# LN1 with the fourth tile's sums on DVE and the first table pieces on ACT's queue; the fourth turn beside the last n1 inverse

## Chip, cores, metric

The kernel runs on one core of a Trainium2 chip. The metric is the device time of one execution in microseconds (us). Engines are named as in the profile: PE is the matrix engine (TensorE), DVE the vector engine, ACT the scalar engine, POOL is GpSimd, SP issues most DMAs.

## The reference, cut to what matters

```python
def _A_ref(x, w_r, w_i):                       # 2048 x 576, bf16
    X = jnp.fft.rfft2(x.astype(jnp.float32)) * (w_r + 1j * w_i)
    return jnp.fft.irfft2(X, s=(S, D)).astype(jnp.bfloat16)
def _B_ref(x, w_gate, w_up, w_down):
    return (gelu(x @ w_gate) * (x @ w_up)) @ w_down
h  = x + _A_ref(layernorm(x), w_r, w_i)
h2 = h + _B_ref(layernorm(h), w_gate, w_up, w_down)
```

The Fourier transforms are matrix products with tables. The scale of the first layer norm (LN1), one number per row, is multiplied into the table of the first transform instead of into x.

## The kernel before

x lies in 16 tiles of 128 rows. LN1 works in five groups of tiles (0-1, 2-3, 4-7, 8-11, 12-15). A tile's statistics come either from DVE (two `bn_stats` of 288 columns and one `bn_aggr`) or, for the tiles in `ACT_TILES`, from two passes of ACT (sum, sum of squares) and two small DVE ops on 128x1 that make a variance of them:

```python
ACT_TILES = (1, 3, 7, 11, 13)
def ln1_var(i):
    for c in range(c0, c1):
        if c in ACT_TILES:   # L446
            P.op(DVE, lambda v: v.scalar_tensor_tensor(TM[:,0,c:c+1], SA[:,0,c:c+1], 1.0/(D*D), SA[:,0,c:c+1], mult, mult) ...)
        else:                # L449
            P.op(DVE, lambda v: v.bn_aggr(MV1[:,c,:], ST1[:,c,:,:]) ...)
    for c in range(c0, c1):
        if c in ACT_TILES:   # L452
            P.op(DVE, lambda v: v.scalar_tensor_tensor(MV1[:,c,1:2], SA[:,1,c:c+1], 1.0/D, TM[:,0,c:c+1], mult, subtract) ...)
```

Then, for each group: root on ACT (`ln1_sqrt`), reciprocal on DVE (`ln1_rs`), the table tile times the scale into `ATS` (`ln1_scale`; groups 2 and 3 in one POOL op, the others on DVE), 10 or 20 matmuls into PSUM (`a_mms`), and five evictions into `U` (`a_evs`, on ACT or DVE). The next transform ("the first transform over U", line L600) needs all of them: its first three matmuls read eviction numbers 0, 1 and 2 of every group, its second half (matmuls 4 to 6) numbers 3 and 4. `idle_mm(n, i)` puts n matmuls without use ahead of group i. After the start comes the middle of the LN1 order:

```python
    # ... groups 0 and 1 cut
    ln1_var(2); ln1_sqrt(2); a_evs(1, ACT, (2, 3, 4)); ln1_tile(8)
    ln1_rs(2);  ln1_scale(2, POOL); idle_mm(7, 2); a_mms(2)
    act_sum(11); act_sq(11); ln1_tile(9); ln1_tile(10); act_sum(13)
    ln1_var(3); ln1_sqrt(3); act_sq(13); ln1_tile(12)
    ln1_rs(3);  ln1_scale(3, POOL); ln1_tile(14)
    a_evs(2, ACT, (0, 1, 2)); ln1_tile(15)
    ln1_var(4); a_evs(2, DVE, (4,)); ln1_sqrt(4); ln1_rs(4); ln1_scale(4, DVE)
    a_evs(2, ACT, (3,)); idle_mm(4, 3); a_mms(3)
    # ... evictions of group 3, a_mms(4), evictions of group 4
```

The other place is the seam between the inverse stage and the FFN. Per tile c, `st_I(c)` (six matmuls, evicted by ACT into `GS`) and `st_N(c-1)` (four matmuls, "n1 inverse") alternate; `turn_pe` transposes one of the first four normalised tiles after tiles 8, 10, 12 and 14; and the last `st_N(15)` comes after the first six FFN matmuls (line L872), which are of another shape (64 instead of 128 rows).

Of the kernel before, what the change touches and what calls it, by code (L numbers as in the profile page):

```python
# [6 lines left out]
ACTF = mybir.ActivationFunctionType  # L7
# [7 lines left out]
NT = 16  # L15
# [280 lines left out]
def _build(nc, A_x, A_w_r, A_w_i, B_w_gate, B_w_up, B_w_down, out):  # L296
    P = Prog(nc)
    T = build_tables()
    dram = {n: nc.inline_tensor(_np_bf16(T[n]), name="c_" + n.lower()) for n in T}
    PE, DVE, ACT, SP, POOL = "pe", "dve", "act", "sp", "pool"  # L300
# [41 lines left out]
    HT0 = sb.alloc("HT0", [128, 5, 512], BF16)  # L342
# [3 lines left out]
    ATB = sb.alloc("ATB", [128, NT, 128], BF16)  # L346
# [21 lines left out]
    PS = nc.alloc_psum_tensor("PS", [128, 4096], F32)  # L368
# [13 lines left out]
    tabs = dram["ATAB"].rearrange("p (c k) -> p c k", c=NT)  # L382
# [1 line left out]
    def x_load(i, c0, c1):  # L384
        P.dma(SP, XO[:, c0:c1, 0:D], xv[:, c0:c1, :], f"x{i}", w=[("X", c) for c in range(c0, c1)])

    def atb_load(i, c0, c1):
        P.dma(SP, ATB[:, c0:c1, :], tabs[:, c0:c1, :], f"atb{i}", w=[("ATB", c) for c in range(c0, c1)])

    x_load(0, 0, 2)  # L390
    x_load(1, 2, 4)
    atb_load(0, 0, 4)
    x_load(2, 4, 8)
    atb_load(1, 4, 8)
    x_load(3, 8, 12)
    x_load(4, 12, 16)
    atb_load(2, 8, 16)
# [27 lines left out]


    GROUPS = ((0, 2), (2, 4), (4, 8), (8, 12), (12, 16))
    ACT_TILES = (1, 3, 7, 11, 13)

    def act_sum(c):  # L430
        P.op(ACT, lambda a, c=c: a.activation(JNK[:, 0, :], XO[:, c, 0:D], ACTF.Identity, accum_out=SA[:, 0, c:c + 1]),
             r=[("X", c)], w=[("SA0", c), "J0"])

    def act_sq(c):
        P.op(ACT, lambda a, c=c: a.activation(JNK[:, 1, :], XO[:, c, 0:D], ACTF.Square, accum_out=SA[:, 1, c:c + 1]),
             r=[("X", c)], w=[("SA1", c), "J1"])

    def ln1_tile(c):
        for h in range(2):
            P.op(DVE, lambda v, c=c, h=h: v.bn_stats(ST1[:, c, h, :], XO[:, c, 288 * h:288 * h + 288]), r=[("X", c)], w=[("ST1", c, h)])  # L440

    def ln1_var(i):
        c0, c1 = GROUPS[i]
        for c in range(c0, c1):
            if c in ACT_TILES:
                P.op(DVE, lambda v, c=c: v.scalar_tensor_tensor(TM[:, 0, c:c + 1], SA[:, 0, c:c + 1], 1.0 / (D * D), SA[:, 0, c:c + 1],  # L446
                                                                op0=ALU.mult, op1=ALU.mult), r=[("SA0", c)], w=[("TM", c)])
            else:
                P.op(DVE, lambda v, c=c: v.bn_aggr(MV1[:, c, :], ST1[:, c, :, :]), r=[("ST1", c, 0), ("ST1", c, 1)], w=[("MV1", c)])  # L449
        for c in range(c0, c1):  # L450
            if c in ACT_TILES:
                P.op(DVE, lambda v, c=c: v.scalar_tensor_tensor(MV1[:, c, 1:2], SA[:, 1, c:c + 1], 1.0 / D, TM[:, 0, c:c + 1],  # L452
                                                                op0=ALU.mult, op1=ALU.subtract), r=[("SA1", c), ("TM", c)], w=[("MV1", c)])

    def ln1_sqrt(i):
        c0, c1 = GROUPS[i]
        P.op(ACT, lambda a, c0=c0, c1=c1: a.activation(RS1[:, c0:c1], MV1[:, c0:c1, 1], ACTF.Sqrt, bias=EPT[:, 0:1]),
             r=[("MV1", c) for c in range(c0, c1)] + ["EPT"], w=[("SD1", i)])

    def ln1_rs(i):  # L460
        c0, c1 = GROUPS[i]
        P.op(DVE, lambda v, c0=c0, c1=c1: v.reciprocal(RS1[:, c0:c1], RS1[:, c0:c1]), r=[("SD1", i)], w=[("RS1", i)])
# [17 lines left out]
    def idle_mm(n, i):  # L480
        b = a_bank(i, AORD[0])
        for _ in range(n):
            P.op(PE, lambda t, b=b: t.matmul(bank(b), ZD[:, 0:128], ZD[:, :], start=True, stop=True), r=["ZD"], w=[("PS", b)])
# [25 lines left out]
    def a_mms(i):  # L509
        for k in AORD:  # L510
            a_mm(i, k)

    def a_evs(i, eng, ks):
        for k in ks:
            a_ev(i, AORD[k], eng)

    P.op(ACT, lambda a: a.activation(SA[:, 0, 0:1], EPT[:, 0:1], ACTF.Sqrt), r=["EPT"], w=[("SA0", 0)])
    idle_mm(11, 0)
    act_sum(1)
    act_sq(1)  # L520
    ln1_tile(0)
    ln1_tile(2)
    act_sum(3)
    ln1_var(0)
    ln1_sqrt(0)
    act_sq(3)
    ln1_rs(0)
    ln1_scale(0, DVE)
    a_mms(0)
    ln1_var(1)  # L530
    ln1_sqrt(1)
    a_evs(0, ACT, (0, 1, 2, 3, 4))
    ln1_rs(1)
    ln1_scale(1, DVE)
    idle_mm(2, 1)
# [3 lines left out]
    ln1_tile(6)  # L539
    act_sum(7)  # L540
    act_sq(7)
    a_evs(1, ACT, (0, 1))
    ln1_var(2)
    ln1_sqrt(2)
    a_evs(1, ACT, (2, 3, 4))
    ln1_tile(8)
    ln1_rs(2)
    ln1_scale(2, POOL)
    idle_mm(7, 2)
    a_mms(2)  # L550
    act_sum(11)
    act_sq(11)
    ln1_tile(9)
    ln1_tile(10)
    act_sum(13)
    ln1_var(3)
    ln1_sqrt(3)
    act_sq(13)
    ln1_tile(12)
    ln1_rs(3)  # L560
    ln1_scale(3, POOL)
    ln1_tile(14)
    a_evs(2, ACT, (0, 1, 2))
    ln1_tile(15)
    ln1_var(4)
    a_evs(2, DVE, (4,))
    ln1_sqrt(4)
    ln1_rs(4)
    ln1_scale(4, DVE)
    a_evs(2, ACT, (3,))  # L570
    idle_mm(4, 3)
    a_mms(3)
    a_evs(3, ACT, (0,))
    a_evs(3, DVE, (1,))
    a_evs(3, ACT, (2,))
    a_evs(3, DVE, (3,))
    a_evs(3, ACT, (4,))
    a_mms(4)
    a_evs(4, DVE, (0,))
    a_evs(4, ACT, (1,))  # L580
    a_evs(4, ACT, (2,))
    a_evs(4, DVE, (3,))
    a_evs(4, ACT, (4,))


    uk = [[("U", i, k) for i in range(len(GROUPS))] + ["Uz"] for k in range(5)]
# [94 lines left out]
    for i in range(NG):  # L681
        P.op(POOL, lambda v, g=GORD[i]: v.tensor_scalar(WS[:, g, 0, :], WS[:, g, 2, :], -1.0, None, op0=ALU.mult),  # L682
             r=[k for k in wkeys[0 if 1 <= GORD[i] < 9 else 1] if k[2] == 1] + ["Wz", ("ATS", NT - 1)], w=[("Wn", i)])
# [40 lines left out]
    vkeys = vk[0] + vk[1] + vk[2]  # L724


    TURN = (8, 10, 12, 14)

    def islot(c):
        return (c + sum(c > t for t in TURN)) % 2  # L730
# [26 lines left out]
    def st_I(c):  # L757
        for h in range(2):
            for i in range(3):
                i_mm(c, h, i)  # L760
        i_ev(c)
# [50 lines left out]
    def turn_pe(c):  # L812
        hs = c % 4
        t0, t1 = 128 * c, 128 * c + 128
        b0 = 2 * ((TURN[c] + 1 + c) % 2)
        for k in range(5):
            b, o = b0 + k // 4, 128 * (k % 4)
            P.op(PE, lambda t, b=b, o=o, k=k, hs=hs: t.matmul(bank(b, 0, 128, o, o + 128), HN[:, hs, 128 * k:128 * k + 128], IDT[:, :], start=True, stop=True),  # L818
                 r=[("HN", hs, 0), ("HN", hs, 1), "IDT"], w=[("PS", b)])
        P.op(ACT, lambda a, t0=t0, t1=t1, b0=b0: a.activation(HT0[:, 0:5, t0:t1], PS[:, b0 * 512:b0 * 512 + 640].rearrange("p (k e) -> p k e", k=5), ACTF.Copy),  # L820
             r=[("PS", b0), ("PS", b0 + 1)], w=[("HT", 0, c, 0)])

    st_I01()
    for c in range(1, NT):
        if c >= 2:
            st_I(c)
        st_N(c - 1)
        if 2 <= c < 6:
            square(c - 2, OS[:, c % 2, :], ("OS", c % 2, 0))
        if c == 5:  # L830
            ln2_a(0)
        if c == 6:
            ln2_b(0)
            ln2_c(0)
            norm(0, DVE)
            norm(1, POOL)
        if c == 7:
            norm(2, DVE)
            norm(3, POOL)
        if c in TURN:  # L840
            turn_pe(TURN.index(c))

    P.alias(ukeys + [(n_, a) for n_ in ("CU", "SU") for a in range(3)], [("WD", j) for j in range(9)])
    for j in range(9):
# [14 lines left out]
    def gu(n):  # L859
        for s_ in range(9 * (n - 1) + LAG, 9 * n + LAG):  # L860
            for half in range(2):
                m, j = divmod(s_ - LAG * half, 9)
                if not 0 <= m < 144:
                    continue
                tb, f = m // 36, m % 36
                o, wt = (ASEQ, BSEQ)[half][j]
                kt = 4 if wt == 8 else wt % 4
                h0 = 64 * half
                HT = HTS[tb % 2]
                b = 2 * (m % 3) + o  # L870
                aft = [half_done[m, o]] if half and (j == 0 or j == 4) else []
                op = P.op(PE, lambda t, h0=h0, kt=kt, wt=wt, f=f, b=b, HT=HT, s=(half == 0 and j in (0, 5)), e=(half == 1 and j in (3, 8)): t.matmul(  # L872
                    bank(b), WGU[h0:h0 + 64, f // 9, wt, 128 * (f % 9):128 * (f % 9) + 128], HT[h0:h0 + 64, kt, :], start=s, stop=e),
                    r=[("HT", tb % 2, i, k) for i in range(4) for k in range(5)] + [("WG", f // 9, i) for i in range(4)],
                    w=[("PS", b)], after=aft)
                if half == 0:
                    half_done[m, o] = op
        m = n - 1
        if m < 0:
            st_N(NT - 1)  # L880
            P.alias(fdead, fnew)
            return
        s2, b0, f = m % 2, 2 * (m % 3), m % 36
        P.op(ACT, lambda a, s2=s2, b0=b0: a.activation(GL[:, s2, :], bank(b0), ACTF.Gelu_apprx_tanh), r=[("PS", b0)], w=[("GL", s2)])  # L884
        P.op(DVE, lambda v, s2=s2, b0=b0, f=f: v.tensor_tensor(AT[:, f, :], GL[:, s2, :], bank(b0 + 1), op=ALU.mult),  # L885
             r=[("GL", s2), ("PS", b0 + 1)], w=[("AT", f)])
# [69 lines left out]
```

## Time and profile before

| | before |
|---|---|
| time, median of 3 runs | 502.13 us (502.11 to 502.88) |
| profiled run, span | 502.82 us, 501.0 us |
| PE busy | 491.8 us, 98% of the span |
| first transform over U: first matmul, second half | 20.53, 21.04 us |
| root of the first and of the last LN1 group | 6.26, 16.80 us |

The span runs from the first to the last instruction; times of instructions count from its start. Starts given to two digits without a fence were read from the single instructions of the trace and are right to 0.01 us. The profiled run is one of the longer ones of its kernel (502.82 us).

The waits of PE, longest in total first (engine, what it wrote, line; for whom it waited: us in total, times, longest):

```profile
PE PS L494 <- POOL ATS L467: 2.7, 2, 2.3
PE PS L494 <- DVE ATS L472: 2.0, 3, 1.6
PE PS L483 <- POOL ZD L377: 1.3, 1, 1.3
PE PS L600 <- DVE U L505: 0.5, 1, 0.5
PE PS L629 <- DVE CUS L613: 0.3, 1, 0.3
```

All the waits in this table lie in the first 23 us, apart from the last row's, at 49 us. So of the places that the change touches, two can make the kernel faster: an earlier start of the first transform, and a shorter seam.

The timeline of DVE around the last root (start, us, line, operation, count, idle time before and who ended it):

```profile
16.29 0.19 DVE L449 BATCH_NORM_AGGREGATE MV<-ST 128x2 f32<-128x12 f32 x1
16.40 0.11 DVE L446 SCALAR_TENSOR_TENSOR TM<-SA 128x1 f32<-128x1 f32 x1
16.42 0.27 DVE L449 BATCH_NORM_AGGREGATE MV<-ST 128x2 f32<-128x12 f32 x2
16.61 0.16 DVE L452 SCALAR_TENSOR_TENSOR MV<-SA,TM 128x1 f32<-128x1 f32 x1
```

The timeline of POOL (start, us, line, operation, count, idle time before and who ended it):

```profile
12.32 1.04 POOL L467 TENSOR_TENSOR ATS<-ATB,RS 128x512 bf16<-128x512 bf16 x1 [7.68 <-DVE RS L462]
15.08 1.04 POOL L467 TENSOR_TENSOR ATS<-ATB,RS 128x512 bf16<-128x512 bf16 x1 [1.72 <-DVE RS L462]
```

The timeline of PE for groups 3 and 4 and the first transform, and at the seam:

```profile
16.18 1.52 PE L494 MATMUL PS<-ATS,XO 128*128 128x128 bf16 x20 [0.38 <-POOL ATS L467]
17.88 0.23 PE L494 MATMUL PS<-ATS,XO 128*128 128x128 bf16 x1 [0.18 <-DVE ATS L472]
18.32 1.68 PE L494 MATMUL PS<-ATS,XO 128*128 128x128 bf16 x19 [0.22 <-DVE ATS L472]
20.53 2.30 PE L600 MATMUL PS<-FT,U 128*128 128x290 bf16 x16 [0.53 <-DVE U L505]
...
73.09 0.44 PE L818 MATMUL PS<-IDT,HN 128*128 128x128 bf16 x5
73.51 0.92 PE L734 MATMUL PS<-DT,V 128*128 128x289 bf16 x6
74.27 0.65 PE L773 MATMUL PS<-GS,IT 128*128 128x288 bf16 x4
74.86 1.47 PE L872 MATMUL PS<-HT,WGU 64*128 64x512 bf16 x6
76.26 0.67 PE L773 MATMUL PS<-GS,IT 128*128 128x288 bf16 x4
```

### The profile page before, as it was taken

To read this page: it belongs to the slowest core of one execution; us is meant where nothing else is said; L and a number is where in the kernel's file an instruction comes from. 1 tells how busy PE (TensorE), PEld (TensorE's weight loads), DVE (VectorE), ACT (ScalarE), POOL (GpSimd) and SP (SyncE) were. 2 spreads that over 40 slices of the span, in tenths; PEclk is the share of its full clock that TensorE was granted. 3 is DMA by queue.
4 is the path that set the end of the run, shared out by engine and by line. 5 is a ranking of instruction groups with operands and counts; after the bars stand their busy time and mean duration, and the time that the engine had idled before them with its cause. 6 is when DMAs were issued, how large, how long until landed. Compare 5 with 4: busy or idle time off the path is not lost.

```text
span 501.0 us, 9981 instructions
## 1 busy us (share of the span) xinstructions
PE 491.8 (98%) x4322; PEld 298.9 (60%) x4323; DVE 182.2 (36%) x390; ACT 158.2 (32%) x296; POOL 39.7 (8%) x49
## 2 busy tenths in 40 slices
PE   6899999999999999999999999999999999999998
PEld 2588774444457764444477744444677544444775
DVE  5899663344421114433311034433201233333111
ACT  7888766653220012332300023232100123233000
POOL 3654290000000000000000000000000000000000
DMA  8779889001100000100000001100000000000000
GB/s 283 167 218 350 279 287 316 2 7 25 26 1 19 18 13 20 22 14 1 2 13 12 19 18 21 23 2 1 1 18 19 13 1 1 1 3 1 12 19 19
DMA packets 25948, 28.64 MB, mean 57 GB/s; under 512 B 11568, under 2 KB 19888, under 8 KB 25776
## 3 DMA queue, kind: packets, MB, share of 16 engines
q1 hardware_dynamic: 23328, 17.39, 12.1%
q0 software_dynamic: 2576, 10.62, 6.2%
q8 instruction: 34, 0.56, 0.5%
q14 instruction: 10, 0.08, 0.1%
HBM read 23.66 MB, written 2.36 MB: 52 GB/s over the span
## 4 chain that ended last, share of the span: by engine, by line
PE 90%; DVE 7%; issue 1%; DMA 1%; ACT 0%; SPq 0%; DVEq 0%
PE PS L872 56%; PE PS L895 28%; PE PS L734 3%; DVE TP L639 2%; PE PS L773 2%; DVE ST L440 1%; DVE ZS L644 1%; DMA XO<-in_A_x_dram 1%; DVE CUS L613 1%; PE PS L600 1%; DVE U L505 0%; DVE ATS L472 0%; DVE CUS L610 0%; PE PS L818 0%; DVE MV L449 0%
## 5 line engine op out<-in xcount | busy, mean ns | idle before, releaser
L872 PE MATMUL PS<-HT,WGU 64*128 64x512 bf16 x2592 | 281.9, 377 | 0.0
L872 PEld LDWEIGHTS PS<-HT,WGU 64*128 64x128 bf16 x2592 | 138.1, 94 | 142.6 <-issue 1.2
L884 ACT ACTIVATE GL<-PS 128x512 bf16<-128x512 f32 x144 | 85.9, 597 | 289.3 <-PE PS L872 289.3
L885 DVE TENSOR_TENSOR AT<-GL,PS 128x512 bf16<-128x512 bf16 x144 | 98.9, 687 | 174.2 <-PE PS L872 172.6
L895 PE MATMUL PS<-WD,AT 128*128 128x288 bf16 (+2 forms) x1152 | 141.8, 286 | 0.0
L895 PEld LDWEIGHTS PS<-WD,AT 128*128 128x128 bf16 x1152 | 110.8, 98 | 31.6 <-issue 1.7
L898 DVE TENSOR_TENSOR OS<-PS,XO 128x288 bf16<-128x288 f32 (+2 forms) x32 | 14.6, 458 | 125.8 <-PE PS L895 125.8
L682 POOL TENSOR_SCALAR WS<-WS 128x290 bf16<-128x290 bf16 x16 | 15.7, 982 | 8.9 <-DMA WS<-in_A_w_i_dram 5.1
L776 DVE SCALAR_TENSOR_TENSOR XO<-PS,XO 128x576 bf16<-128x576 f32 x16 | 12.1, 756 | 8.4 <-PE PS L773 8.4
L600 PE MATMUL PS<-FT,U 128*128 128x290 bf16 x96 | 14.4, 287 | 0.5 <-DVE U L505 0.5
L734 PE MATMUL PS<-DT,V 128*128 128x289 bf16 x96 | 14.6, 287 | 0.0
L662 PE MATMUL PS<-VT,ZS 128*128 128x256 bf16 x102 | 13.5, 272 | 0.1
L639 DVE TENSOR_TENSOR TP<-YS,WS 128x580 bf16<-128x580 bf16 (+2 forms) x32 | 13.5, 462 | 0.3 <-issue 0.3
L673 ACT ACTIVATE V<-PS 128x768 bf16<-128x768 f32 x15 | 11.9, 811 | 0.8 <-PE PS L662 0.6
L494 PE MATMUL PS<-ATS,XO 128*128 128x128 bf16 (+1 forms) x80 | 7.1, 223 | 4.6 <-POOL ATS L467 2.7
L632 ACT ACTIVATE YS<-PS 128x578 bf16<-128x578 f32 x16 | 10.5, 654 | 3.5 <-PE PS L629 3.3
L743 ACT ACTIVATE GS<-PS 128x578 bf16<-128x578 f32 x15 | 9.8, 654 | 4.2 <-PE PS L734 4.1
L629 PE MATMUL PS<-CUS,BT 128*128 128x289 bf16 (+2 forms) x96 | 10.7, 247 | 0.3 <-DVE CUS L613 0.3
L600 PEld LDWEIGHTS PS<-FT,U 128*128 128x128 bf16 x96 | 9.2, 98 | 3.0 <-issue 0.7
L734 PEld LDWEIGHTS PS<-DT,V 128*128 128x128 bf16 x96 | 8.9, 97 | 3.4 <-issue 0.3
L764 ACT ACTIVATE OS<-XO 128x576 bf16<-128x576 bf16 x16 | 10.8, 674 | 0.0
L773 PE MATMUL PS<-GS,IT 128*128 128x288 bf16 x64 | 10.5, 285 | 0.0
(59 smaller groups left out, 156.4 us busy)
## 6 DMA issues: line engine op xcount, KB each, us to landing
WD<-in_B_w_down_dram POOLq DMA_DIRECT2D x9, 576.0 KB, 9.1
WGU<-in_B_w_up_dram SPq DMA_DIRECT2D x4, 1152.0 KB, 9.4
WGU<-in_B_w_gate_dram POOLq DMA_DIRECT2D x4, 1152.0 KB, 10.0
out_dram<-OS SPq DMA_DIRECT2D x30, 72.0 KB, 1.6
XO<-in_A_x_dram SPq DMA_DIRECT2D x3, 576.0 KB, 7.4
IT<-c_itab SPq DMA_DIRECT2D x1, 1024.0 KB, 7.1
HT<-HN SPq DMA_TRANSPOSE x60, 2.4
XO<-in_A_x_dram SPq DMA_DIRECT2D x2, 288.0 KB, 3.4
```

The lines of the kernel that those rows point to most:

```text
L600: P.op(PE, lambda t, b=b, o=o, dt=dt, us=us, g=g: t.matmul(bank(b, 0, 128, 0, 2 * HK), U[:, us, g, :, :], FT[:, o, dt, :], start=(dt == 0) ...
L639: P.op(DVE, lambda v: v.tensor_tensor(out, YS[:, sl, :, q0:q1], WS[:, g, w_, q0:q1], op=ALU.mult), r=[("Y", sl), ("Wn", i), "Yz", "Zz"] + ...
L662: P.op(PE, lambda t, b=b, o=o, zp=zp, lhs=lhs, sp_=sp_, m=m, n=len(parts): t.matmul(bank(b, 0, 128, o, o + 256), lhs, VT[:, sp_, zp, :], s ...
L682: P.op(POOL, lambda v, g=GORD[i]: v.tensor_scalar(WS[:, g, 0, :], WS[:, g, 2, :], -1.0, None, op0=ALU.mult), r=[k for k in wkeys[0 if 1 <= ...
L734: P.op(PE, lambda t, b=b, h=h, i=i, kt=kt, c=c: t.matmul(bank(b, 0, 128, 0, K2), V[:, kt, c, :, :], DT[:, 3 * h + i, 0:K2], start=(i == 0) ...
L773: P.op(PE, lambda t, b=b, h=h, i=i, c=c, rhs=rhs: t.matmul(bank(b, 0, 128, 0, 288), IT[:, h * i, c, :], rhs, start=(i == 0), stop=(i == 1) ...
L776: P.op(DVE, lambda v, x2=x2, c=c, sl=sl: v.scalar_tensor_tensor(x2, banks(4 + 2 * sl, 2, 288), 1.0, x2, op0=ALU.mult, op1=ALU.add, accum_o ...
L872: op = P.op(PE, lambda t, h0=h0, kt=kt, wt=wt, f=f, b=b, HT=HT, s=(half == 0 and j in (0, 5)), e=(half == 1 and j in (3, 8)): t.matmul(ban ...
L884: P.op(ACT, lambda a, s2=s2, b0=b0: a.activation(GL[:, s2, :], bank(b0), ACTF.Gelu_apprx_tanh), r=[("PS", b0)], w=[("GL", s2)])
L885: P.op(DVE, lambda v, s2=s2, b0=b0, f=f: v.tensor_tensor(AT[:, f, :], GL[:, s2, :], bank(b0 + 1), op=ALU.mult), r=[("GL", s2), ("PS", b0 + ...
L895: P.op(PE, lambda t, b=b, d0=d0, d1=d1, f=f, p=p: t.matmul(bank(b, 0, 128, 0, d1 - d0), AT[:, f, 128 * p:128 * p + 128], WD[:, f, d0:d1], ...
L898: P.op(DVE, lambda v, b=b, d0=d0, d1=d1, p=p, c=c: v.tensor_tensor(OS[:, p % 2, d0:d1], bank(b, 0, 128, 0, d1 - d0), XO[:, c, d0:d1], op=A ...
```

## The change

Its intent: take tile 3 off ACT, issue the first tables on ACT's own queue so that x loads follow one another on SP's, rebalance the evictions, and let the fourth turn fill the wait for the last eviction of the inverse stage instead of letting FFN matmuls do it.

```diff
-    atb_load(0, 0, 4)            # was on SP between the x loads; likewise atb_load(1, 4, 8)
+    atb_load(0, 0, 4, ACT)       # now on ACT, after its first small op
+    atb_load(1, 4, 8, ACT)
-    ACT_TILES = (1, 3, 7, 11, 13)
+    ACT_TILES = (1, 7, 11, 13)
+    ln1_tile(3, (0,))            # one half before ln1_rs(0), the other before ln1_var(1)
 ... (groups 0 to 2 cut)
     act_sum(11)
     act_sq(11)
+    ln1_tile(8, (1,))
     ln1_tile(9)
     ln1_tile(10)
+    ln1_tile(12)
+    ln1_var(3)
     act_sum(13)
-    ln1_var(3)
+    act_sq(13)
     ln1_sqrt(3)
-    act_sq(13)
-    ln1_tile(12)
+    ln1_tile(14)
     ln1_rs(3)
     ln1_scale(3, POOL)
-    ln1_tile(14)
+    ln1_tile(15)
     a_evs(2, ACT, (0, 1, 2))
-    ln1_tile(15)
     ln1_var(4)
-    a_evs(2, DVE, (4,))
     ln1_sqrt(4)
+    a_evs(2, ACT, (3, 4))
+    idle_mm(4, 3)
+    a_mms(3)
     ln1_rs(4)
     ln1_scale(4, DVE)
 ... (evictions of groups 3 and 4 in another order; still ACT 3+3, DVE 2+2 of ten)
-    TURN = (8, 10, 12, 14)
+    TURN = (8, 10, 12, 15)
 ... (turn 3 evicted by DVE instead of ACT, and emitted between st_I(15) and st_N(14))
+    st_N(NT - 1)                 # now before the FFN; removed from after its first six matmuls
```

More of the change, by code (lines that the diff above doesn't have):

```diff
@@ L385, in x_load, with atb_load @@
         P.dma(SP, XO[:, c0:c1, 0:D], xv[:, c0:c1, :], f"x{i}", w=[("X", c) for c in range(c0, c1)])
-    def atb_load(i, c0, c1):
-        P.dma(SP, ATB[:, c0:c1, :], tabs[:, c0:c1, :], f"atb{i}", w=[("ATB", c) for c in range(c0, c1)])
+    def atb_load(i, c0, c1, eng=SP):
+        P.dma(eng, ATB[:, c0:c1, :], tabs[:, c0:c1, :], f"atb{i}", w=[("ATB", c) for c in range(c0, c1)])
     x_load(0, 0, 2)
     x_load(1, 2, 4)
-    atb_load(0, 0, 4)
     x_load(2, 4, 8)
-    atb_load(1, 4, 8)
     x_load(3, 8, 12)
@@ L436, in act_sq, with ln1_tile @@
              r=[("X", c)], w=[("SA1", c), "J1"])
-    def ln1_tile(c):
-        for h in range(2):
+    def ln1_tile(c, hs=(0, 1)):
+        for h in hs:
             P.op(DVE, lambda v, c=c, h=h: v.bn_stats(ST1[:, c, h, :], XO[:, c, 288 * h:288 * h + 288]), r=[("X", c)], w=[("ST1", c, h)])
@@ L522, in _build @@
     ln1_tile(2)
-    act_sum(3)
     ln1_var(0)
     ln1_sqrt(0)
-    act_sq(3)
+    ln1_tile(3, (0,))
     ln1_rs(0)
@@ L529, in _build @@
     a_mms(0)
+    ln1_tile(3, (1,))
     ln1_var(1)
+    a_evs(0, ACT, (0,))
     ln1_sqrt(1)
-    a_evs(0, ACT, (0, 1, 2, 3, 4))
+    a_evs(0, ACT, (1, 2, 3, 4))
     ln1_rs(1)
@@ L541, in _build @@
     act_sq(7)
-    a_evs(1, ACT, (0, 1))
+    a_evs(1, ACT, (0, 1, 2))
     ln1_var(2)
     ln1_sqrt(2)
-    a_evs(1, ACT, (2, 3, 4))
-    ln1_tile(8)
+    a_evs(1, ACT, (3, 4))
+    ln1_tile(8, (0,))
     ln1_rs(2)
@@ L552, in _build @@
     act_sq(11)
+    ln1_tile(8, (1,))
     ln1_tile(9)
     ln1_tile(10)
+    ln1_tile(12)
+    ln1_var(3)
     act_sum(13)
-    ln1_var(3)
+    act_sq(13)
     ln1_sqrt(3)
-    act_sq(13)
-    ln1_tile(12)
+    ln1_tile(14)
     ln1_rs(3)
     ln1_scale(3, POOL)
-    ln1_tile(14)
+    ln1_tile(15)
     a_evs(2, ACT, (0, 1, 2))
-    ln1_tile(15)
     ln1_var(4)
-    a_evs(2, DVE, (4,))
     ln1_sqrt(4)
+    a_evs(2, ACT, (3, 4))
+    idle_mm(4, 3)
+    a_mms(3)
     ln1_rs(4)
     ln1_scale(4, DVE)
-    a_evs(2, ACT, (3,))
-    idle_mm(4, 3)
-    a_mms(3)
-    a_evs(3, ACT, (0,))
-    a_evs(3, DVE, (1,))
-    a_evs(3, ACT, (2,))
-    a_evs(3, DVE, (3,))
+    a_evs(3, ACT, (0, 1))
+    a_evs(3, DVE, (2, 3))
     a_evs(3, ACT, (4,))
     a_mms(4)
-    a_evs(4, DVE, (0,))
-    a_evs(4, ACT, (1,))
-    a_evs(4, ACT, (2,))
-    a_evs(4, DVE, (3,))
-    a_evs(4, ACT, (4,))
+    a_evs(4, ACT, (0, 1))
+    a_evs(4, DVE, (2,))
+    a_evs(4, ACT, (3,))
+    a_evs(4, DVE, (4,))
     uk = [[("U", i, k) for i in range(len(GROUPS))] + ["Uz"] for k in range(5)]
@@ L819, in turn_pe @@
                  r=[("HN", hs, 0), ("HN", hs, 1), "IDT"], w=[("PS", b)])
-        P.op(ACT, lambda a, t0=t0, t1=t1, b0=b0: a.activation(HT0[:, 0:5, t0:t1], PS[:, b0 * 512:b0 * 512 + 640].rearrange("p (k e) -> p k e", k=5), ACTF.Copy),
-             r=[("PS", b0), ("PS", b0 + 1)], w=[("HT", 0, c, 0)])
+        src = PS[:, b0 * 512:b0 * 512 + 640].rearrange("p (k e) -> p k e", k=5)
+        if c == 3:
+            P.op(DVE, lambda v, t0=t0, t1=t1, src=src: v.tensor_copy(HT0[:, 0:5, t0:t1], src), r=[("PS", b0), ("PS", b0 + 1)], w=[("HT", 0, c, 0)])
+        else:
+            P.op(ACT, lambda a, t0=t0, t1=t1, src=src: a.activation(HT0[:, 0:5, t0:t1], src, ACTF.Copy), r=[("PS", b0), ("PS", b0 + 1)], w=[("HT", 0, c, 0)])
     st_I01()
@@ L826, in _build @@
             st_I(c)
+        if c == NT - 1:
+            turn_pe(3)
         st_N(c - 1)
@@ L839, in _build @@
             norm(3, POOL)
-        if c in TURN:
+        if c in TURN[0:3]:
             turn_pe(TURN.index(c))
+    st_N(NT - 1)
     P.alias(ukeys + [(n_, a) for n_ in ("CU", "SU") for a in range(3)], [("WD", j) for j in range(9)])
@@ L879, in gu @@
         if m < 0:
-            st_N(NT - 1)
             P.alias(fdead, fnew)
```

## The prediction

> **What bounds the kernel now.** The span is 501.0 us and the matrix engine is busy 98% of it (page, part 1). Its 9 us of idle time lie nearly all in the first 21 us (wait table: 2.7 us on tables scaled by POOL, 2.0 us by DVE). The chain of waits runs over DVE from 5 to 52 us, then over the matrix engine. So the change can act at two places: the first transform over U, whose halves start at 20.53 and 21.04 us (timeline), and the seam between inverse stage and FFN (73 to 77 us).
>
> **Head: what moves.** Tile 3 leaves ACT (sum and square, 1.33 us) for DVE (two statistics at 0.36 us, minus two small ops: about +0.5 us). One 128x512 eviction of group 2 leaves DVE (0.60 us) for ACT (0.48 us). ACT issues two table loads (0.43 us each) while it waits for x anyway (idle 2.2 to 3.8 us).
>
> **Head: critical path.** I replayed both queues with durations of the trace. Half of tile 3 fits in DVE's 0.36 us wait for the first root; the other half delays group 1's root by 0.2 us, and DVE then works without a gap until the last variance: its root on ACT moves from 16.80 to about 17.07 us. Group 3's root moves from 14.4 to 15.2 and its POOL scaling from 15.1 to 16.1 us. After the last root ACT has eight evictions (0.48 us each) instead of seven, DVE four as before: ACT's last needed one ends near 21.2 us, where DVE's ended at 20.98. So the second half of the first transform starts at about 21.3 instead of 21.04 us: +0.25 us, which DVE, saturated until 52 us, passes on.
>
> A further risk: [...] Tables on ACT's queue would share with tiles 2 and 3 of x, which landed at 4.98 us and on which the chain hangs: estimate 0 to 0.3 us (eight 46-ns packets per engine). No trace of before shows it.
>
> **Seam.** Six FFN matmuls stand between two inverse groups; each change of tile shape costs a gap of 0.09 us. Moving the last inverse group ahead removes two: -0.19 us. The fourth turn fills the last eviction of G (0.2 + 0.65 us, against 0.42 + 0.49 us of turn and inverse matmuls). The turn's eviction on DVE (0.8 us, estimated from 0.68 us per 128x512) ends as the last inverse group ends: wait 0 to 0.1 us.
>
> **Sum.** 502.1 + 0.25 + 0.1 (DMA risk) - 0.19 = about 502.2 us. Range 501.4 to 502.9, which also covers the 0.8 us spread of the runs of before. Faster by over 2%: 0.01; within 2%: 0.98; slower: 0.01.
>
> **What the profile would show.** First statistics of tile 2 at 5.0 us (5.3 if the queues collide); second root at 7.9; POOL scalings at 12.2 and 16.1; last root near 17.1; ACT unbroken until 21.1; first transform's second half near 21.3; the seam 0.2 us shorter, no idle between last inverse group and FFN.
>
> **What would make it wrong.** x landing earlier as the tables left SP's queue (gain only if DVE waited for it; after tile 2 it does not); DVE's eviction of the turn slower than 0.9 us; ACT and DVE interleaving better than replayed, so that the first transform starts before 20.5 us.

(The 0 to 0.3 us for the DMA risk, and the 5.3 us further down, are the author's estimate; its 46 ns is the median of the 256 packets of 1 KB of the first two table loads in the trace of before, eight for each load and engine if 16 engines share them evenly. The sum: 502.1 + 0.25 + 0.1 - 0.19 = 502.26, given as about 502.2 us. The gap of 0.09 us is in the trace of before: at each of the three changes of shape between 74.64 and 76.86 us the next matmul starts 0.09 to 0.10 us later than at the pace of its predecessors.)

## More of the kernel before

The small op L446 takes 0.11 us. It runs at 16.40; POOL's second scaling ended at 15.08 + 1.04 = 16.12.

## The result, and the profile after

The changed kernel took 502.95 us (median of 4 runs, 502.89 to 503.98), before 502.12 (502.07 to 502.88): ratio 1.0018, interval 1.0000 to 1.0035. (A ratio is the mean time of one kernel's fast runs over that of the other's of the same rounds, so not quite the ratio of the medians.) So +0.83 us where about +0.1 was predicted (its terms add to +0.16). Executions over 1.5% slower than the fastest of the same kernel are left out of the means. The interval of this pair touches 1; the same kernel gave 1.0015 (1.0001 to 1.0029) again in a_after. The profiled run after is again an unlucky one, of 503.98 us with a mean clock of 0.993, span 502.2.

DVE around the last root, after (the groups that answer to L449, L446, L449, L452):

```profile
16.24 0.19 DVE L447 BATCH_NORM_AGGREGATE MV<-ST 128x2 f32<-128x12 f32 x1
16.35 0.46 DVE L444 SCALAR_TENSOR_TENSOR TM<-SA 128x1 f32<-128x1 f32 x1
16.73 0.27 DVE L447 BATCH_NORM_AGGREGATE MV<-ST 128x2 f32<-128x12 f32 x2
16.92 0.10 DVE L450 SCALAR_TENSOR_TENSOR MV<-SA,TM 128x1 f32<-128x1 f32 x1
```

POOL after:

```profile
11.92 1.04 POOL L465 TENSOR_TENSOR ATS<-ATB,RS 128x512 bf16<-128x512 bf16 x1 [7.28 <-DVE RS L460]
15.76 1.04 POOL L465 TENSOR_TENSOR ATS<-ATB,RS 128x512 bf16<-128x512 bf16 x1 [2.80 <-DVE RS L460]
```

The same small op on tile 13 takes 0.46 us instead of 0.11, and everything on DVE behind it is 0.35 us later. It ends at 16.81 us, POOL's scaling at 16.79.

The waits of PE after, and its timeline for groups 3 and 4 and the seam:

```profile
PE PS L492 <- POOL ATS L465: 2.8, 2, 2.0
PE PS L492 <- DVE ATS L470: 1.5, 1, 1.5
PE PS L481 <- POOL ZD L377: 1.3, 1, 1.3
```

```profile
16.85 4.81 PE L492 MATMUL PS<-ATS,XO 128*128 128x128 bf16 x40 [0.76 <-POOL ATS L465]
21.50 1.37 PE L598 MATMUL PS<-FT,U 128*128 128x290 bf16 x6
...
74.46 0.91 PE L732 MATMUL PS<-DT,V 128*128 128x289 bf16 x6
75.21 0.44 PE L816 MATMUL PS<-IDT,HN 128*128 128x128 bf16 x5
75.49 1.30 PE L771 MATMUL PS<-GS,IT 128*128 128x288 bf16 x8
76.72 0.60 PE L876 MATMUL PS<-HT,WGU 64*128 64x512 bf16 x2
```

PE waits less than before in the wait table and yet is later: the 40 matmuls take 4.81 us, where before 20 took 1.52. They start 107 ns apart instead of 56. PE's busy time hides it; the clock shows it. Busy time by stretch of the trace after (us from the span's start, length, then PE, its weight loads, DVE, ACT, POOL, the granted PE clock, DMA share, GB/s):

```profile
11.14:14.55 3.41, 1.53 (x21) 1.26 (x22) 3.41 (x14) 3.28 (x10) 1.04 (x1) 1.00 1.10 329
14.55:17.96 3.41, 2.65 (x14) 1.21 (x13) 2.83 (x15) 2.85 (x9) 1.04 (x1) 0.50 0.95 195
```

The clock was halved from 14.55 to 21.38 us in this run. At the seam the gain is as predicted: counted from the start of the third last n1 group (tile 13), the seventh FFN matmul starts after 4.05 us, before after 4.25.

So there are three suspects for the head: the small op beside POOL, the clock, and the arrival of x with the tables on another queue; and the rival that the replay of the queues itself was wrong (tile 3's statistics cost more than +0.25 us).

### The profile page after: what moved, and what is told of

It is laid out like the page before. It is cut to its first block, busy times and chain, and to the rows that moved or that the text cites. A ratio compares the mean times of both kernels' runs of the same rounds, so it can differ in the third digit from the quotient of the medians.

```text
span 502.2 us, 9977 instructions
## 1 busy us (share of the span) xinstructions
PE 493.5 (98%) x4323; PEld 300.5 (60%) x4323; DVE 183.7 (37%) x391; ACT 156.9 (31%) x292; POOL 39.5 (8%) x49
## 4 chain that ended last, share of the span: by engine, by line
PE 91%; DVE 7%; issue 1%; DMA 1%; POOL 0%; ACT 0%; SPq 0%; DVEq 0%; POOLq 0%
PE PS L876 56%; PE PS L898 28%; PE PS L732 3%; DVE TP L637 2%; PE PS L771 2%; DVE ST L438 1%; DVE ZS L642 1%; PE PS L492 1%; DMA XO<-in_A_x_dram 1%; PE PS L598 1%; DVE CUS L611 1%; DVE CUS L608 0%; PE PS L816 0%; POOL ATS L465 0%; PE PS L627 0%
## 5 line engine op out<-in xcount | busy, mean ns | idle before, releaser
L492 PE MATMUL PS<-ATS,XO 128*128 128x128 bf16 (+1 forms) x80 | 8.5, 265 | 4.4 <-POOL ATS L465 2.8
L492 PEld LDWEIGHTS PS<-ATS,XO 128*128 128x128 bf16 (+1 forms) x80 | 6.3, 123 | 8.2 <-POOL ATS L465 4.2
L438 DVE BATCH_NORM_STATS2 ST<-XO 128x6 f32<-128x288 bf16 x24 | 9.4, 446 | 3.8 <-DMA XO<-in_A_x_dram 3.8
```

Of the source, the lines that this page charges most:

```text
L438: P.op(DVE, lambda v, c=c, h=h: v.bn_stats(ST1[:, c, h, :], XO[:, c, 288 * h:288 * h + 288]), r=[("X", c)], w=[("ST1", c, h)])
L492: P.op(PE, lambda t, b=b, w=w, o=o, c=c, k=k: t.matmul(bank(b, 0, w, o, o + 128), XO[:, c, TILES[k]], ATS[:, c, :], start=True, stop=True) ...
```

## Experiments

Every kernel was timed in five rounds against the kernel before on the same chip and gave a correct result. Intervals of ratios are about ±0.0013, that is ±0.65 us, so a single comparison of 0.3 us is not resolved by time alone. The two columns ahead of the last count from the first root, which takes the arrival of the first tiles of x out. All starts are in us.

| run | median us (range) | before, same chip | ratio | first root | last root, after the first | second half of the first transform, after the first root | half clock in the traced run |
|---|---|---|---|---|---|---|---|
| trace of before | 502.13 (502.11-502.88) | | | 6.26 | 10.54 | 14.78 | none |
| a_before | 502.33 (502.03-502.37) | 502.16 | 1.0001 | 5.74 | 10.74 | 14.98 | 12.87-16.28 |
| trace of after | 502.95 (502.89-503.98) | 502.12 | 1.0018 | 5.91 | 11.15 | 16.16 | 14.55-21.38 |
| a_head | 503.35 (502.82-504.21) | 502.16 | 1.0027 | 5.91 | 11.14 | 16.15 | 14.51-21.34 |
| a_seam | 502.02 (501.94-502.32) | 502.16 | 0.9999 | 5.76 | 10.71 | 14.95 | 14.39-17.80 |
| b_queue | 502.48 (502.47-502.83) | 502.16 | 1.0008 | 5.78 | 10.68 | 14.93 | 12.80-16.22 |
| b_after_spq | 502.69 (502.55-503.76) | 502.16 | 1.0014 | 5.52 | 11.14 | 15.39 | none |
| b_after_warm | 502.81 (502.57-502.91) | 502.16 | 1.0012 | 5.71 | 11.15 | 15.39 | none |
| b_seam_warm | 501.84 (501.75-502.26) | 502.16 | 0.9995 | 5.63 | 10.56 | 14.80 | none |
| c_stt | 502.36 (502.25-502.52) | 502.20 | 1.0004 | 5.70 | 10.84 | 15.08 | none |
| c_order | 502.50 (502.35-503.22) | 502.20 | 1.0008 | 5.73 | 11.07 | 15.31 | none |
| c_dummy | 502.97 (502.75-503.31) | 502.20 | 1.0016 | 5.57 | 11.00 | 15.36 | none |
| c_cold | 502.76 (502.04-502.92) | 502.20 | 1.0007 | 5.61 | 10.53 | 14.78 | 11.63-18.45 |
| d_mended | 502.38 (502.33-502.51) | 502.40 | 1.0000 | 5.75 | 10.84 | 15.09 | none |

The arrival of later tiles of x still enters these two columns, before the third root (that of group 2). Counted from the third root to the second half of the first transform, the traces fall into clean classes:

| order | traces | third root to second half, us |
|---|---|---|
| before, at full clock or with a half-clock stretch that ends by 18.5 us | before, a_before, a_seam, b_queue, b_seam_warm, c_cold | 9.63 to 9.65 |
| changed, full clock | b_after_spq, b_after_warm | 10.04 |
| changed, half clock to 21.3 us | after, a_head | 10.80 |
| changed, full clock, tile 13's small op clear of POOL | c_stt, c_order, d_mended | 9.73 to 9.74 |
| before, with the superfluous small op | c_dummy | 10.24 |

**a_before**: the kernel before, unchanged.

> The kernel before, unchanged, for the spread of times and a second trace. Its times so far are 502.07, 502.11, 502.13 and 502.88 us, and the one trace at hand is of a 502.82 us run. Theory of two states: the trace of a 502.1 us run differs from the one at hand by about 0.7 us somewhere before the first transform over U (which started at 20.53 us there), and no difference after it. Rival: the 0.7 us is outside the span (the span stays 501.0 us while the time says 502.1).

The spread was 502.03 to 502.37 us, span 500.5 in the traced run. Here x arrived sooner: the first statistics of tile 2 started at 4.48 us, directly behind tile 0's, against 5.01 in the trace at hand, where DVE waited 0.36 us for them (last column). That put the first root 0.52 us earlier, and the first transform's second half 0.32 us earlier (20.72 us), as a later wait for x took 0.2 back (see b_seam_warm). So the trace on which the prediction was worked out had a late x, and "21.04 us" is not typical of before; the rest of the 0.5 us between the two runs lies in later stages and was not followed. The theory of one 0.7 us step held in part only.

```profile
3.83 0.82 DVE L440 BATCH_NORM_STATS2 ST<-XO 128x6 f32<-128x288 bf16 x2 [3.83 <-DMA XO<-in_A_x_dram]
5.01 0.82 DVE L440 BATCH_NORM_STATS2 ST<-XO 128x6 f32<-128x288 bf16 x2 [0.36 <-DMA XO<-in_A_x_dram]
```

(the trace of before), and a_before, with all four in one row:

```profile
3.73 1.56 DVE L440 BATCH_NORM_STATS2 ST<-XO 128x6 f32<-128x288 bf16 x4 [3.73 <-DMA XO<-in_A_x_dram]
```

**a_after**: the changed kernel, unchanged.

> The changed kernel, unchanged. The trace at hand has a granted TensorE clock of 0.5 from 14.8 to 21.6 us, and the first transform started 0.97 us later than before and its second half 1.03 us later. Theory A (order of evictions): at full clock throughout, the second half starts at about 21.3 to 21.6 us and the run takes 502.3 to 502.9 us. Rival B (clock): the half-clock stretch comes with this order in most runs, and is most of the loss; then the trace shows it again and the time stays near 503.

Its fast runs took 502.77 to 502.99 us. The traced run fell into a slow state (739.7 us, clock 0.656 throughout). The other four runs had mean clocks of 0.997 or 1.000: in a span of 501 us, 0.997 is one half-clock stretch of 3.4 us (3.4 x 0.5 / 501 = 0.0034; the trace of a_before has 0.997 and one of 3.41 us) and 0.993 is two (the trace after has 0.993 and 6.83 us). So rival B falls as the main cause: the long half-clock stretch is not in most runs, it makes the 504 us of some.

**a_head** and **a_seam**: the two halves of the diff by themselves.

> Only the LN1 part and the table loads of the change, the seam as before. Expected 0.2 us more than the whole change, whose seam was 0.21 us shorter in the trace: 503.1 us, ratio to before near 1.002. If the seam's gain is not real, it equals the whole change, 502.9.

> Only the seam of the change (fourth turn after the last inverse transform, its eviction on DVE, last n1 group before the FFN). Expected 0.2 us less than before: 501.9 us beside 502.1; in the trace no idle time of the matrix engine between the last inverse group and the FFN. Rival: 0, if what is saved comes back as a wait for the turn's eviction.

The head alone took 503.35 us; the interval of its ratio (1.0015 to 1.0040) is the clearest. Its two runs at 0.993 took 504.17 and 504.21 us, its three others 502.82 to 503.35: the long half-clock stretch costs about 1 us where it falls so. The seam alone gave -0.14 us in the median; in its trace the seventh FFN matmul stands 0.2 us nearer, as in the trace after. The rows below merge gaps under 0.15 us. Inside the x8, the second n1 group starts 0.63 us after the first, where groups take 0.49 us elsewhere (for instance 73.97 to 74.46 us in the trace after): it still waits about 0.13 us, in the trace after for the last eviction of the inverse stage (ACT). The step to the FFN behind it has no gap beyond that of the change of shape (0.09 to 0.10 us in the traces of before and after):

```profile
73.75 1.30 PE L773 MATMUL PS<-GS,IT 128*128 128x288 bf16 x8
74.98 2.34 PE L878 MATMUL PS<-HT,WGU 64*128 64x512 bf16 x14
```

**b_queue**: before, with only the two table loads on ACT's queue. **b_after_spq**: the whole change, with only these loads back on SP's.

> The kernel before with one part of the change: the first two table loads on ACT's queue. Theory: tiles 2 and 3 of x then share the DMA engines with the tables; the first statistics of tile 2 start at 4.65 to 4.75 us (4.48 in the undisturbed trace of before), the chain behind it moves by 0.2 us and the time is 502.3. Rival: the 0.2 us was chance of arrival; start at 4.48, time 502.1 or, with SP's later loads 0.95 us sooner, less.

> The whole change except the queue: tables on SP's queue between the x loads as before. Theory: first statistics of tile 2 at 4.48 us again, group 3's scaling on POOL still near 15.6 us, last root near 16.9, second half of the first transform near 21.2 at full clock; 0.2 us faster than the whole change at equal clock, 502.7 us. If the queue was all of the loss it is 501.9; if it was none, 502.95.

Alone the queue change cost 0.32 us by the medians, taken back it gave 0.26 us (502.95 to 502.69). In the traces tile 2's statistics waited for x, beyond the 0.37 us that tile 0's second half needs, 0.15 (after), 0.22 (a_head), 0.17 (b_queue), 0.03 to 0.09 us (the other fast runs with the tables on ACT's queue), and 0 to 0.05 us in those with SP's, except the first trace of before. The tables did run beside x: in the trace after, from 3.9 to 4.4 us, the packets of ACT's queue took 52.7% of the time of the 16 DMA engines and those of SP's 43.1%. a_head shows such a wait as a row of its own:

```profile
3.68 0.82 DVE L438 BATCH_NORM_STATS2 ST<-XO 128x6 f32<-128x288 bf16 x2 [3.68 <-DMA XO<-in_A_x_dram]
4.65 0.82 DVE L438 BATCH_NORM_STATS2 ST<-XO 128x6 f32<-128x288 bf16 x2
```

So the sign was as the theory had it, and the size up to 0.3 us by the times, which is inside the interval of each ratio; the traces account for 0.2 of it at most, and the first trace of before, with its tables on SP's queue, waited longer (0.43 us) than any of them. In b_queue's trace the first transform stood where it stood in a_before (20.71 and 20.72 us); its other 0.17 us came in the spectral stage, whose length (second half of the first transform to first n1 inverse) varies from 33.93 to 34.22 us between the traces in which it starts at full clock. Why is left open. b_after_spq also shows that the small op of tile 13 stays slow (0.46 us) and the 15.39 us remain: the queue is one cost, not the cost.

**b_after_warm**: the whole change with more filler matmuls.

```diff
-    idle_mm(7, 2)
+    idle_mm(15, 2)
-    idle_mm(4, 3)
+    idle_mm(10, 3)
```

> The whole change with 15 and 10 instead of 7 and 4 filler matmuls ahead of groups 2 and 3, which end before the tables arrive. Theory: the granted clock of 0.5 from 14.5 to 21.4 us follows idle time of the matrix engine (2.0 us before group 2, 0.8 us before group 3); with the fillers the trace shows clock 1.0 there, matmuls of groups 3 and 4 start 56 ns apart instead of 107, the second half of the first transform starts at about 21.3 us instead of 22.07, and the times lose their tail above 503: median 502.6, none over 502.9. Rival: the clock falls for another reason[...], then the half clock is still there or the fillers run at half rate and delay group 3: 503 or more.

No run had a clock below 1.000, and none took over 502.91 us. PE in the trace:

```profile
16.66 3.00 PE L492 MATMUL PS<-ATS,XO 128*128 128x128 bf16 x40 [0.16 <-POOL ATS L465]
```

The 40 matmuls took 3.00 us instead of 4.81, and the second half of the first transform came at 15.39 us after the first root instead of 16.16. So the half clock went with the idle time of PE, which ahead of groups 2 and 3 was 2.02 and 0.76 us in the trace after and is 0.29 and 0.16 us here, and a long half-clock stretch costs 0.77 us here. The length of one gap does not decide it: the trace of before has 2.28 us ahead of group 2 and no half clock. (The extra fillers themselves cost nothing: b_after_spq, with the old ones but at full clock by luck, has the same 15.39.) But the median fell by 0.14 us only, as most runs never had the long stretch; and that 0.14 is not shown to be the clock, as runs of the unchanged after with a mean clock of 1.000 took 502.92 to 502.98 us.

In the traces the half-clock stretches were 3.41 or 6.83 us long, to 0.01 us, and began at 11.63, 12.80, 12.87, 14.39, 14.51 or 14.55 us: in a_before at 12.87 and in a_seam, whose LN1 code is the same, at 14.39, and in the trace of before not at all. What sets their start was not shown. As it differs between runs of the same code, the tail of the times is a matter of luck.

**b_seam_warm**: before, with the seam and with fillers (16 and 6).

> The kernel before with the seam of the change and 16 and 6 instead of 7 and 4 fillers: a candidate. The half-clock window of before (12.9 to 16.3 or 14.4 to 17.8 us) should vanish. Theory: it cost nothing there, because ACT still has statistics to do while group 2's matmuls run slowly; so 501.95 us, as the seam alone. Rival: it cost something; then up to 0.3 us less than the seam alone.

501.84 us against 502.16, the fastest of all versions; the interval of its ratio (0.9982 to 1.0009) still holds 1. Its 14.80 us after the first root is what the order of before takes at full clock; a_before and a_seam, each with one short half-clock stretch, took 14.98 and 14.95. But the clock is not what made the difference: it arose before the third root (5.17 us after the first in b_seam_warm, 5.34 in a_before, 5.31 in a_seam), and so before the half-clock stretches began, because DVE stood still for x ahead of tile 4's statistics. The two scalings end at 8.14 us in a_before and at 8.07 in b_seam_warm:

```profile
7.72 0.42 DVE L472 TENSOR_SCALAR ATS<-ATB,RS 128x128 bf16<-128x128 bf16 x2
8.25 2.26 DVE L440 BATCH_NORM_STATS2 ST<-XO 128x6 f32<-128x288 bf16 x6
```

(a_before), and b_seam_warm, where the statistics follow without a pause (instructions of DVE overlap a little in the profile):

```profile
7.65 0.42 DVE L472 TENSOR_SCALAR ATS<-ATB,RS 128x128 bf16<-128x128 bf16 x2
7.98 2.25 DVE L440 BATCH_NORM_STATS2 ST<-XO 128x6 f32<-128x288 bf16 x6
```

From the third root on, the traces with and without a short stretch agree (9.64 and 9.63 us). So a short stretch cost nothing in the traces, as the theory had it, and the lower time of this run is not explained by it.

**c_stt**: b_after_warm, with the two small ops of tile 13 moved on DVE out of POOL's way.

```diff
-    ln1_tile(14)                       # and the two small ops of tile 13 in ln1_var(4)
+    TM[13] = SA0[13] * SA0[13] / D**2   # same op as before, on DVE
+    ln1_tile(14, (0,))
+    MV1[13] = SA1[13] / D - TM[13]
+    ln1_tile(14, (1,))
     ln1_rs(3)
```

> The whole change with the longer fillers, and tile 13's two small variance ops (two inputs each) moved on DVE from after tile 15 to around the first half of tile 14, before POOL's scaling of group 3 starts. Theory: in all five traces of the changed order that op took 0.46 us instead of 0.10 and ended 13 to 16 ns after POOL's op[...]; moved out of POOL's way it takes 0.10 us, the last root starts about 0.45 us sooner after the first one (10.7 instead of 11.15 us), the second half of the first transform at 14.95 instead of 15.39 us after the first root, and the time falls by 0.4 us from the 502.8 of the longer fillers. Rival: the 0.35 us belong to the place in the instruction stream[...] or to tile 13's data; then they show up at another op and the time stays.

DVE in c_stt (L564 and L567 are the moved ops; POOL's scaling started at 15.68 us):

```profile
14.52 0.15 DVE L564 SCALAR_TENSOR_TENSOR TM<-SA 128x1 f32<-128x1 f32 x1
14.59 0.45 DVE L438 BATCH_NORM_STATS2 ST<-XO 128x6 f32<-128x288 bf16 x1
14.96 0.14 DVE L567 SCALAR_TENSOR_TENSOR MV<-SA,TM 128x1 f32<-128x1 f32 x1
```

The small ops took 0.15 and 0.14 us. The last root came 0.31 us sooner after the first, the second half of the first transform at 15.08 instead of 15.39 us, the time fell from 502.81 to 502.36 (0.16 over before, where it was 0.65 over it). The theory had hoped for 0.13 us more in the trace.

**c_dummy**: before, with one superfluous op of the same form where POOL scales.

```diff
     ln1_tile(14)
+    P.op(DVE, lambda v, c=13: v.scalar_tensor_tensor(TM[:, 1, c:c + 1], SA[:, 0, c:c + 1], 1.0 / (D * D), SA[:, 0, c:c + 1], ...))
```

> The kernel before with one superfluous small op of the same form (128x1, two inputs) on DVE after tile 14, which falls in POOL's scaling of group 3 (14.75 to 15.79 us). [...]it takes about 0.55 us instead of 0.10 and ends 15 ns after POOL's op; all of DVE behind it moves by about 0.5 us, the second half of the first transform starts 15.4 to 15.5 us after the first root instead of 14.95, and the time grows by 0.4 to 0.5 us. Rival: it takes 0.10 us and the time grows by 0.1 or nothing.

(The theory: beside POOL's scaling this op ends only with POOL's op, as tile 13's did in the traces of the changed order.) POOL and then DVE in c_dummy:

```profile
14.36 1.04 POOL L467 TENSOR_TENSOR ATS<-ATB,RS 128x512 bf16<-128x512 bf16 x1 [1.72 <-DVE RS L462]
```

```profile
14.85 0.56 DVE L563 SCALAR_TENSOR_TENSOR TM<-SA 128x1 f32<-128x1 f32 x1
15.34 0.81 DVE L440 BATCH_NORM_STATS2 ST<-XO 128x6 f32<-128x288 bf16 x2
16.07 0.18 DVE L449 BATCH_NORM_AGGREGATE MV<-ST 128x2 f32<-128x12 f32 x1
16.18 0.10 DVE L446 SCALAR_TENSOR_TENSOR TM<-SA 128x1 f32<-128x1 f32 x1
```

The superfluous op took 0.56 us, ended 14 ns after POOL's, and its twin 1.3 us later took 0.10. The last root came at 11.00 us after the first (10.56 in the order of before at full clock, b_seam_warm), the second half of the first transform at 15.36 (14.80), and the time rose by 0.77 us, more than the 0.4 to 0.5 expected and than the 0.56 of the trace. This settles it: in six traces (this one and five of the changed order, one of them the slow a_after, whose small op took the same 0.46 us) the op ended 13 to 16 ns after POOL's. DVE's two statistics of tile 14, which have one input each and ran from 14.15 us on, mostly beside POOL's op, took 0.79 us, no longer than elsewhere (0.81). So an op of 128 numbers with two inputs was not done until POOL's op of 1.04 us was; what holds it up was not shown.

**c_order**: b_after_warm, with group 3 in the order of before (and 7 fillers ahead of it).

> The whole change with fillers (15 and 7), but group 3 in the order of before: its variance ahead of tile 12, its root ahead of tile 13's square. Tile 3 stays on DVE. Theory: POOL's scaling of group 3 starts at 14.9 instead of 15.6 us and ends before the small op of tile 13, which takes 0.10 us again; last root about 0.35 us sooner, second half of the first transform 15.05 us after the first root, time 502.45. Rival: tile 3's statistics on DVE are the loss; then it stays at 15.39 us and 502.8.

POOL's scaling started at 15.08 us and had ended at 16.12 when the small op came, which took 0.10 us:

```profile
16.39 0.10 DVE L444 SCALAR_TENSOR_TENSOR TM<-SA 128x1 f32<-128x1 f32 x1
```

The numbers after the first root fell by 0.08 us only, because in this trace DVE stood still for 0.2 us earlier, ahead of tile 4's statistics (no row between 7.92 + 0.42 and 8.48 us), for x. Counted from the third root, which comes after that pause, c_order takes 9.74 us, as c_stt does (9.73), where b_after_warm takes 10.04. Its time, 502.50 us, is near the expected 502.45. So the order of group 3 is what moved POOL's scaling onto the small op, and tile 3 is not the main loss.

**c_cold**: before, without the fillers ahead of groups 2 and 3.

> The kernel before without the fillers ahead of groups 2 and 3 (the opposite of the longer fillers). Clock theory: the half-clock stretch grows from 3.4 to 6.8 us or more, from about 12.9 or 14.4 to 20 us, matmuls of groups 3 and 4 start 107 ns apart, and the second half of the first transform starts 0.5 to 1.0 us later (15.5 to 16 us after the first root): 502.7 to 503.2 us. Rival: the clock doesn't follow the matrix engine's idle time and nothing changes.

All five runs had a clock of 0.993, so the half-clock stretch did double in every run. The traced run lost nothing by it: the stretch ended at 18.45 us, before most of group 4's matmuls, and the second half came 14.78 us after the first root. The times fall in two heaps, 502.04 and 502.17, and 502.76 to 502.92 us. That the slow heap is where the stretch reaches further, as in the trace after, was argued and not shown, as no slow run was traced. The expected loss in the trace was a miss.

**d_mended**: the whole change with all three costs taken out (fillers, small ops moved, tables on SP's queue).

> The whole change with its three unforeseen costs taken out together: fillers 15 and 10, tile 13's small ops moved out of POOL's way, and the tables back on SP's queue. Theory: the costs add up, and what remains is tile 3 on DVE (second half of the first transform about 15.05 us after the first root, against 14.80 in before with fillers) and the seam's 0.2 us: 502.15 us, equal to before within 0.1, tile 2's statistics directly behind tile 0's (no wait for x), clock 1.0. Rival: the queue cost nothing in this version, then 502.36 as with the tables on ACT; or a fourth cost is left, then more.

502.38 us, against 502.40 for before on that chip, which was 0.2 us slower than the others: ratio 1.0000 (0.9986 to 1.0014). Relative to before it is 0.18 us better than c_stt. Tile 2's statistics waited 0.05 us, the second half came at 15.09 us. No fourth cost is needed. (One run of before on that chip took 1048.29 us; it is a slow one.)

## Why the prediction was wrong, point by point

- **Seam, -0.19 us: right.** The traces of after and a_seam show -0.2; DVE's eviction of the turn took 0.83 us (0.8 estimated) and made no wait.
- **Evictions and tile 3 on DVE, +0.25 us: right, to 0.03 us.** With the other costs out, c_stt and d_mended take 15.08 and 15.09 us from the first root to the second half, the order of before at full clock takes 14.80: +0.28.
- **The last root "moves from 16.80 to about 17.07": the step that failed.** It did come at 17.06 us, but in a run whose first root was 0.35 us earlier. Counted from the first root the replay gave 10.81 us, and the traces after show 11.15. The replay took every DVE duration over unchanged from the trace of before. The reordered POOL scaling (predicted at 16.1, found at 15.76 us, as predicted from the first root) now lay over tile 13's small op, which waited 0.35 us for it. The prediction named this move of POOL's and did not ask what DVE runs beside it. Missing term: +0.31 us in the trace (c_stt; c_order +0.30 counted from the third root), up to 0.45 by the times.
- **DMA risk, +0.1 us: of the sign foreseen, perhaps too small.** By the times it was about 0.2 to 0.3 us (b_queue +0.32, b_after_spq -0.26, d_mended against c_stt -0.18; each inside its interval), of which the traces show at most 0.2 as a wait of tile 2's statistics. What makes it, no run isolates.
- **"ACT unbroken until 21.1", "second half near 21.3": wrong in the traced run, by the clock.** 22.07 us was measured. Group 3's later tables left PE idle for 0.76 us (0.38 in before), the clock stayed halved for 6.83 us (3.41 in a_before), and ACT waited for PE. At full clock (b_after_warm) ACT was unbroken, as predicted, from the last root to its last eviction at 21.06 us. The prediction didn't treat the clock at all. In an unlucky run it counts about 1 us; in the median nothing is shown to be its doing (see b_after_warm).
- **The sum.** Terms that were missing or too small: 0.31 (small op beside POOL) + 0.15 (queue beyond 0.1, middle of its estimates, not resolved) = +0.46, with the +0.16 of the predicted terms +0.62; measured +0.83. The remaining 0.2 us stays open; it is of the size by which runs differ.

## What to carry to other kernels

When an order of work is replayed on paper, durations don't travel with the ops: list for every moved POOL op which DVE ops now run beside it, however small they are (here an op of 128x1 with two inputs took 0.46 and 0.56 us instead of 0.10, while statistics with one input took 0.79 us as elsewhere), and ask which stretches of the matrix engine's idle time grow. Where runs differ by as much as the change is worth, count from an event inside the trace (here a root) rather than from the span's start, look for waits for input behind that event too, and take a second trace of the kernel before. Filler matmuls that end just before the real ones arrive (PE idle for 0.29 and 0.16 us in b_after_warm) took the long half-clock stretch away here: none of the 25 runs with longer fillers had a mean clock of 0.993, as 4 of the 18 fast runs of after, a_after, a_head and b_after_spq had.
